# Eight lower halves of each weight formed on TensorE as a difference, and the second batch's variance on ScalarE

## The chip, the cores and the metric

One core of a Trainium2 chip runs the whole problem. The metric is the device time of one execution, in microseconds (us). Engines are named as the profile names them: PE (TensorE, with PEld for its weight loads), DVE (VectorE), ACT (ScalarE), POOL (GpSimd), SP (the queue that starts DMAs).

## The reference

Eight batches of landmark attention (8 heads, 576 tokens, 64 columns, 32 landmarks) are computed, their outputs laid side by side as x (576 x 512 per batch), and x goes through a Fourier mix and a two-layer perceptron:

```
mixed = real(fft(fft(x, axis=1), axis=2))
u  = x + mixed
un = (u - mean(u)) / sqrt(var(u) + 1e-6)          # per token
out = u + relu(un @ w_ch1) @ w_ch2                # 512 -> 2048 -> 512
```

## The kernel before, in words

Three Python generators write the program: `attention` (batch after batch), `weights` and `mlp`. A loop in `run` hands them control by a clock kept by cost estimates. PE executes in the order in which they write (L881); the order on DVE, ACT and POOL is made by the framework's scheduler. Each engine runs its list strictly in order, so an instruction that waits holds up all behind it.

**Weights.** w1 and w2 come as 64-bit floats and are cut into 16 pieces each, [128, 512]. For a piece, ACT makes the magnitude (`prepare`), DVE puts the number together in three instructions (L287 to L289), and ACT takes its maximum (`bound`). When a weight's 16 maxima are there, `scale` finds one power of two for it: a maximum on DVE, a transpose and a small product on PE, and five tiny DVE instructions that end in `wsc`. Then `halve` cuts each piece into an upper and a lower fp16 half (`split`, L209):

```
self.A.activation(hi, src, AF.Copy, scale=scale)                               # ACT
self.V.scalar_tensor_tensor(lo, src, scale, hi, ALU.mult, ALU.subtract)        # DVE
```

Piece f is kept as fp32 in slot f + 1 of `whole[w]`, and its two halves are written into slot f: the halves of piece f + 1 overwrite piece f, so ACT's hi of the next piece waits for DVE's lo of this one. w1 is halved while w2 is still being put together, one piece for one; w2 is halved after all that.

**Perceptron.** Tokens go in 18 chunks of 256. For a chunk, `mlp` runs eight steps over pairs of pieces of w1: 24 matmuls (three fp16 products of halves, 256 columns each) into a PSUM tile `h` of the pool `ps_h`, which has two banks (PSH = 2); ACT takes the relu's upper half out of it, DVE the lower (L852, L853). `second` then multiplies such a step's h with two pieces of w2: 12 matmuls of 512 columns into two accumulators `acc`. The first chunk needs a pair of w1 as soon as it is halved, and the second layer a pair of w2.

**Norm.** `norm` makes mean and variance of the u tiles: for batch 0 on ACT with sums that accumulate (`nm` is the negative mean), for all others on DVE with `bn_stats` and `bn_aggr`. Then come a power on POOL, un on DVE, its fp16 halves on ACT and POOL, and DMA transposes into unT.

Almost all instructions are recorded by one line (L121 for ACT, DVE and POOL, L197 for PE), so rows are told apart by tile names. `w<-w,wsc` is a half of a piece (hi on ACT, lo on DVE), `h<-h` and `mid<-h` empty a step of the perceptron, `w<-w,row`, `w<-big,row` and `row<-...` put pieces together.

Of the kernel before, what the change touches and what calls it, by code (L numbers as in the profile page):

```python
# [10 lines left out]
F32 = mybir.dt.float32  # L11
F16 = mybir.dt.float16
I32 = mybir.dt.int32
AF = mybir.ActivationFunctionType
ALU = mybir.AluOpType
AX = mybir.AxisListType

P = 128
H, S, D, LM, DM, DF = 8, 576, 64, 32, 512, 2048
NF = DF // P  # L20
# [105 lines left out]
class Kernel:  # L126
    def __init__(self, ctx, tc, NB, q, k, v, w1, w2, t1, t1t, t2, diag, mask, out):
        self.tc, self.nc, self.NB = tc, tc.nc, NB
        self.q, self.k, self.v, self.w1, self.w2, self.out = q, k, v, w1, w2, out
        nc = self.nc  # L130
# [10 lines left out]
        def const(src, shape, dtype, name):  # L141
            t = self.cp.tile(shape, dtype, name=name)
            nc.sync.dma_start(t, src)
            return t

        self.wraw, self.raw_there = [], []
        self.whole = [self.cp.tile([P, NF + 1, 512], F32, name=f"w{w}") for w in range(2)]
        self.mask = const(mask, [P, 6], F32, "mask")
# [7 lines left out]
        self.ones_bd = self.cp.tile([P, 4, 32], F32, name="ones_bd")  # L156
        nc.vector.tensor_copy(self.ones_bd, self.mask4.unsqueeze(2).broadcast_to([P, 4, 32]))
        self.mhalf = self.cp.tile([P, 2], F32, name="mhalf")
        nc.vector.memset(self.mhalf, -0.5)
# [73 lines left out]
    def weights(self):  # L233
        nc = self.nc
        V, A = self.V, self.A
        whole = self.whole
        slots = [[t[:, i] for i in range(NF + 1)] for t in whole]
        am = [self.cp.tile([P, NF], F32, name=f"wmax{w}") for w in range(2)]
        hl = [[t.bitcast(F16).rearrange("p (y m) -> p y m", y=2) for t in ss] for ss in slots]
        self.w1s = [t.rearrange("p y (c f) -> p y c f", c=KT) for t in hl[0]]  # L240
        self.w2s = hl[1]
        sc = self.cp.tile([P, 3], F32, name="wsc")
        pieces = [(w, f) for w in range(2) for f in range(NF)]
        mags = []
# [8 lines left out]
        def bound(i):  # L253

            w, f = pieces[i]
            A.activation(mags[i], slots[w][f + 1], AF.Abs, accum_out=am[w][:, f : f + 1])

        es = []

        def scale(w):  # L260
            a2 = self.small(1, "wm2")
            V.tensor_reduce(a2, am[w], AX.X, ALU.max)
            yield self.till(a2)
            e, r = yield from self.pow2(a2, 1, f"wp{w}")
            es.append(e)
            V.tensor_scalar(sc[:, w : w + 1], r[:, 0:1], (2.0**6, 2.0**14)[w], None, ALU.mult)

        def halve():
            w, f = pieces[sum(self.split_w)]
            self.split(hl[w][f][:, 0], hl[w][f][:, 1], slots[w][f + 1], sc[:, w : w + 1])  # L270
            self.split_w[w] = f + 1

        for i, (w, f) in enumerate(pieces):
# [11 lines left out]
            top, low = rv[:, :, 1], rv[:, :, 0]  # L285
            x, dst = mags[i].bitcast(I32), slots[w][f + 1]
            V.tensor_scalar(x, x, 3, None, ALU.logical_shift_left)  # L287
# [10 lines left out]
            if es:  # L298
                halve()
                yield max(0.0, max(self.V.free, self.G.free) - self.now - WT)  # L300
# [3 lines left out]
        self.inv2 = sc[:, 2:3]  # L304
        while sum(self.split_w) < 2 * NF:
            halve()
            yield max(0.0, max(self.V.free, self.A.free) - self.now - WT)
# [441 lines left out]
    def norm(self, b, uts):  # L749
        nc, V = self.nc, self.V  # L750
        n = len(uts)
        st, mv = self.sm.tile([P, 2, 6], F32, name="bn"), self.sm.tile([P, 2, 2], F32, name="mv")
        ve, r0, t, r1 = (self.small(2, x)[:, 0:n] for x in ("ve", "r0", "rt", "r1"))
        if b == 0:
            junk = self.row(512)
# [25 lines left out]
        for j, ut in enumerate(uts):  # L781
            i = self.ntile
# [10 lines left out]
            hl = self.row(1024, F16).rearrange("p (y d) -> p y d", y=2)  # L793
# [77 lines left out]
    def run(self):  # L871
# [3 lines left out]
        self.ulive, self.ufree, self.first_done, self.seconds, self.folded = 0, [], 0, 0, -1  # L875
        self.split_w, self.decoded = [0, 0], 0
        self.threads = []
# [83 lines left out]
```

## Time and profile before

| what | value |
|---|---|
| median of 3 runs | 1067.77 us (1065.95 to 1068.18) |
| the profiled execution, its time | 1067.68 us |
| its span, first to last instruction | 1065.9 us |
| PE busy | 981.1 us, 92% |
| DVE busy | 614.0 us, 58% |
| ACT busy | 351.7 us, 33% |
| mean granted PE clock | 0.96 |

Busy shares are means over stages that differ: PE is not full in the first 200 us and full from there on, while DVE is nearly full only in those first 200 us. The 1.8 us between time and span lie outside the instructions.

### The profile page before, as it was taken

What the parts mean: (1) busy time and instruction counts of PE and PEld (TensorE: products, weight loads), DVE (VectorE), ACT (ScalarE), POOL (GpSimd) and SP (SyncE); (2) the same over time, 40 slices, a digit from 0 to 9 for tenths busy, and PEclk for the clock granted to TensorE, in tenths of its full rate; (3) what the DMA queues carried; (4) which work ended last, traced back from release to release, by engine and by line L of the source; (5) the groups of instructions that cost most, each with busy time, mean ns of one, the idle gap of its engine ahead of it and who ended that gap; (6) DMA issues with size and microseconds to landing.
All of it is one profiled execution on the core that took longest, in us unless ns stands there. A gap on an engine that the chain in (4) does not pass through costs nothing.

```text
span 1065.9 us, 19548 instructions
## 1 busy us (share of the span) xinstructions
PE 981.1 (92%) x8008; PEld 681.0 (64%) x8008; DVE 614.0 (58%) x1655; ACT 351.7 (33%) x791; POOL 126.6 (12%) x137
## 2 busy tenths in 40 slices
PE   1553779999999999999999999999999999999998
PEld 0442645677776677766776777667766677766665
DVE  7889888768553476446746574567451654341111
ACT  4566755324221333124322332243312332111110
POOL 0101101021101030110302030104010030110000
PEclk8556989999999999999999999999999999999999
DMA  9824402221401022111502050114111010120000
GB/s 328 311 83 129 141 25 91 70 42 39 152 21 35 26 80 103 21 31 21 179 4 50 11 164 19 40 21 129 64 41 21 21 23 20 21 50 16 5 21 20
DMA packets 85994, 71.70 MB, mean 67 GB/s; under 512 B 56336, under 2 KB 74768, under 8 KB 85776
## 3 DMA queue, kind: packets, MB, share of 16 engines
q1 hardware_dynamic: 85904, 70.45, 22.1%
q8 instruction: 63, 1.03, 0.4%
q14 instruction: 27, 0.22, 0.1%
HBM read 48.02 MB, written 9.44 MB: 54 GB/s over the span
## 4 chain that ended last, share of the span: by engine, by line
PE 86%; DVE 8%; issue 2%; ACT 2%; DMA 1%; POOL 0%; SPq 0%; ACTq 0%; DVEq 0%
PE acc L197 34%; PE h L197 34%; PE at L197 16%; DVE w L121 2%; DVE row L121 2%; DVE mid L121 1%; PE at L202 1%; ACT row L121 1%; DVE lm L121 1%; DMA big<-q_dram 0%; ACT mid L121 0%; DVE asum L121 0%; DVE u L121 0%; DVE RE L121 0%; POOL row L121 0%
## 5 line engine op out<-in xcount | busy, mean ns | idle before, releaser
L197 PE MATMUL h<-unT,w 128*128 128x256 f16 x3456 | 413.5, 274 | 20.3 <-DMA unT<-row 11.5
L197 PEld LDWEIGHTS <-w 128*128 128x128 f16 x3456 | 336.2, 98 | 92.8 <-issue 19.5
L197 PE MATMUL acc<-w,h 128*128 128x512 f16 x1680 | 394.8, 379 | 0.0
L197 PEld LDWEIGHTS <-h 128*128 128x128 f16 x1680 | 161.9, 98 | 160.5 <-issue 3.4
L121 DVE SCALAR_TENSOR_TENSOR h<-h 128x512 f16<-128x512 f32 x140 | 96.5, 689 | 247.5 <-ACT h L121 247.0
L121 ACT ACTIVATE h<-h 128x512 f16<-128x512 f32 x140 | 83.4, 596 | 367.9 <-PE h L197 367.5
L121 POOL TENSOR_TENSOR r<-ve,mhalf 128x2 f32<-128x2 f32 (+1 forms) x20 | 13.7, 683 | 446.7 <-DVE ve L121 446.7
L121 POOL TENSOR_TENSOR row<-row 128x512 f16<-128x512 f32 (+1 forms) x44 | 47.3, 1089 | 44.0 <-ACT row L121 44.0
L197 PEld LDWEIGHTS <-mid 128*128 128x128 f16 x432 | 40.2, 103 | 17.7 <-issue 9.0
L197 PEld LDWEIGHTS <-big 128*128 128x128 f16 (+1 forms) x768 | 41.3, 106 | 13.6 <-issue 2.4
L121 POOL TENSOR_TENSOR mid<-mid,asum 128x512 f32<-128x512 f32 x14 | 15.1, 1080 | 272.2 <-issue 134.5
L121 DVE TENSOR_REDUCE lm<-big 128x32 f32<-128x576 f32 (+1 forms) x48 | 44.2, 945 | 3.3 <-DMA big<-k_dram 3.2
L121 DVE SCALAR_TENSOR_TENSOR row<-at,scw,row 128x262 f32<-128x262 f32 (+1 forms) x48 | 21.4, 486 | 41.4 <-ACT row L121 27.2
L121 ACT CAST row<-row 128x512 f16<-128x512 f32 (+1 forms) x44 | 23.2, 557 | 64.5 <-DVE row L121 63.9
L121 ACT ACTIVATE row<-w 128x512 f32<-128x512 f32 x54 | 33.8, 641 | 22.8 <-DVE w L121 12.4
L197 PE MATMUL at<-RE,E 128*128 128x96 f32 (+1 forms) x192 | 31.1, 288 | 9.0 <-DVE RE L121 9.0
L121 DVE SCALAR_TENSOR_TENSOR u<-at,scw,row 128x128 f32<-128x128 f32 (+3 forms) x120 | 38.9, 389 | 0.0
L121 POOL TENSOR_TENSOR mid<-mid 128x256 f32<-128x256 f32 (+1 forms) x32 | 31.5, 987 | 61.5 <-DVE mid L121 54.0
L197 PEld LDWEIGHTS at<-RE,E 128*128 128x128 f32 x192 | 28.6, 205 | 15.3 <-issue 6.2
L121 DVE TENSOR_TENSOR mid<-mid 128x256 f32<-128x256 f32 x48 | 34.5, 743 | 1.6 <-POOL mid L121 1.4
L197 PE MATMUL at<-mid,big 128*128 128x262 f16 (+1 forms) x288 | 34.3, 293 | 0.0
L121 DVE SCALAR_TENSOR_TENSOR u<-acc,wsc,u 128x512 f32<-128x512 f32 x36 | 26.7, 745 | 11.5 <-PE acc L197 11.3
(167 smaller groups left out, 955.6 us busy)
## 6 DMA issues: line engine op xcount, KB each, us to landing
w<-w_dram SPq DMA_DIRECT2D x22, 512.0 KB, 8.9
big<-v_dram SPq DMA_DIRECT2D x16, 640.0 KB, 9.2
big<-q_dram SPq DMA_DIRECT2D x16, 584.0 KB, 5.2
big<-k_dram SPq DMA_DIRECT2D x16, 576.0 KB, 4.2
out_dram<-u SPq DMA_DIRECT2D x36, 256.0 KB, 2.0
big<-w_dram SPq DMA_DIRECT2D x10, 512.0 KB, 8.2
unT<-row SPq DMA_TRANSPOSE x72, 2.4
t<-t_dram SPq DMA_DIRECT2D x1, 1048.0 KB, 9.2
```

The source lines that it names most:

```text
L121: return call(out, *args, **kw)
L197: self.nc.tensor.matmul(out, a, b, start=start, stop=stop, skip_group_check=True)
L202: self.nc.tensor.transpose(out, a, ident)
```

## The change

Pieces with an even number are halved as before. For an odd piece ACT makes hi, and PE forms the scaled difference in a tile of `ps_h`: the fp32 piece times the identity scaled by `wsc` (`scaled[w]`, tile `wid`), plus hi times minus the identity (`minus`, fp16). ACT copies that tile out as lo. For w1 the difference of an odd piece is written into the program one piece later (`left`), for w2 at once. w1's slots are one further apart (piece f in slot f + 2). Batch 1's mean and variance are made on ACT as those of batch 0.

```diff
@@ -144,7 +144,7 @@
             return t
 
         self.wraw, self.raw_there = [], []
-        self.whole = [self.cp.tile([P, NF + 1, 512], F32, name=f"w{w}") for w in range(2)]
+        self.whole = [self.cp.tile([P, NF + 2 - w, 512], F32, name=f"w{w}") for w in range(2)]
         self.mask = const(mask, [P, 6], F32, "mask")
         self.load(0)
         self.mask4, self.mask2 = self.mask[:, 0:4], self.mask[:, 4:6]
@@ -155,6 +155,8 @@
         nc.vector.memset(self.ones, 1.0)
         self.ones_bd = self.cp.tile([P, 4, 32], F32, name="ones_bd")
         nc.vector.tensor_copy(self.ones_bd, self.mask4.unsqueeze(2).broadcast_to([P, 4, 32]))
+        self.minus = self.cp.tile([P, P], F16, name="minus")
+        nc.vector.tensor_scalar(self.minus, self.ident, -1.0, None, ALU.mult)
         self.mhalf = self.cp.tile([P, 2], F32, name="mhalf")
         nc.vector.memset(self.mhalf, -0.5)
 
@@ -234,7 +236,7 @@
         nc = self.nc
         V, A = self.V, self.A
         whole = self.whole
-        slots = [[t[:, i] for i in range(NF + 1)] for t in whole]
+        slots = [[t[:, i] for i in range(NF + 2 - w)] for w, t in enumerate(whole)]
         am = [self.cp.tile([P, NF], F32, name=f"wmax{w}") for w in range(2)]
         hl = [[t.bitcast(F16).rearrange("p (y m) -> p y m", y=2) for t in ss] for ss in slots]
         self.w1s = [t.rearrange("p y (c f) -> p y c f", c=KT) for t in hl[0]]
...
-            A.activation(mags[i], slots[w][f + 1], AF.Abs, accum_out=am[w][:, f : f + 1])
+            A.activation(mags[i], slots[w][f + 2 - w], AF.Abs, accum_out=am[w][:, f : f + 1])
...
@@ -264,11 +266,33 @@
             e, r = yield from self.pow2(a2, 1, f"wp{w}")
             es.append(e)
             V.tensor_scalar(sc[:, w : w + 1], r[:, 0:1], (2.0**6, 2.0**14)[w], None, ALU.mult)
+            V.tensor_scalar(scaled[w], self.ident, sc[:, w : w + 1], None, ALU.mult)
+            self.begun[w] = 0
+
+        scaled = [self.cp.tile([P, P], F32, name=f"wid{w}") for w in range(2)]
+        left = []
 
         def halve():
-            w, f = pieces[sum(self.split_w)]
-            self.split(hl[w][f][:, 0], hl[w][f][:, 1], slots[w][f + 1], sc[:, w : w + 1])
-            self.split_w[w] = f + 1
+
+
+            w = 0 if self.begun[0] < NF else 1
+            f = self.begun[w]
+            hi, lo, src = hl[w][f][:, 0], hl[w][f][:, 1], slots[w][f + 2 - w]
+            if f % 2 == 0:
+                self.split(hi, lo, src, sc[:, w : w + 1])
+            else:
+                A.activation(hi, src, AF.Copy, scale=sc[:, w : w + 1])
+            self.begun[w] += 1
+            left.append((w, f, hi, lo, src))
+            while left and (left[0][1] % 2 == 0 or len(left) > 1 - left[0][0] or self.begun[0] == NF):
+                w, f, hi, lo, src = left.pop(0)
+                if f % 2:
+                    yield self.till(hi)
+                    ps = self.ps_h.tile([P, 512], F32, name="h")
+                    self.mm(ps, scaled[w], src, True, False)
+                    self.mm(ps, self.minus, hi, False, True)
+                    A.copy(lo, ps)
+                self.split_w[w] = f + 1
 
         for i, (w, f) in enumerate(pieces):
             while len(mags) < min(2 * NF, i + 1 + PREP):
...
-            x, dst = mags[i].bitcast(I32), slots[w][f + 1]
+            x, dst = mags[i].bitcast(I32), slots[w][f + 2 - w]
...
@@ -296,14 +320,14 @@
             if i == NF:
                 yield from scale(0)
             if es:
-                halve()
+                yield from halve()
                 yield max(0.0, max(self.V.free, self.G.free) - self.now - WT)
         bound(2 * NF - 1)
         yield from scale(1)
         V.tensor_scalar(sc[:, 2:3], es[0][:, 0:1], 2.0**-19, es[1][:, 0:1], ALU.mult, ALU.mult)
         self.inv2 = sc[:, 2:3]
-        while sum(self.split_w) < 2 * NF:
-            halve()
+        while sum(self.begun) < 2 * NF:
+            yield from halve()
             yield max(0.0, max(self.V.free, self.A.free) - self.now - WT)
 
     def arrival(self, mb):
@@ -751,7 +775,7 @@
         n = len(uts)
         st, mv = self.sm.tile([P, 2, 6], F32, name="bn"), self.sm.tile([P, 2, 2], F32, name="mv")
         ve, r0, t, r1 = (self.small(2, x)[:, 0:n] for x in ("ve", "r0", "rt", "r1"))
-        if b == 0:
+        if b < 2:
             junk = self.row(512)
             nm = self.small(2, "nm")[:, 0:n]
             for j, ut in enumerate(uts):
```

What follows are rows of the two programs' order. Numbers tell buffers apart; `w0_73` is the tile of w1's slots, `w1_74` that of w2's, `[waits ...]` names the engine (or DMA queue) whose signal an instruction waits for.

PE before, in the first chunk, from the end of one step of the first layer (`h_1079`) to the start of the next (`h_1116`):

```order
L197 LDWEIGHTS w0_73
L197 MATMUL h_1079<-unT_868,w0_73 128x256
L197 LDWEIGHTS w0_73 [waits Activation_49]
L197 MATMUL h_1116<-unT_868,w0_73 128x256 [waits DVE_49]
L197 LDWEIGHTS w0_73
L197 MATMUL h_1116<-unT_868,w0_73 128x256
```

PE of the changed kernel, at the same kind of place, from step `h_1200` to step `h_1243`:

```order
L199 LDWEIGHTS w0_73
L199 MATMUL h_1200<-unT_870,w0_73 128x256
L199 MATMUL h_1235<-w0_73,wid0_137 128x512 [waits DVE_49]
L199 LDWEIGHTS minus_108
L199 MATMUL h_1235<-w0_73,minus_108 128x512 [waits Activation_49]
L199 LDWEIGHTS w0_73
L199 MATMUL h_1243<-unT_870,w0_73 128x256 [waits DVE_49]
L199 LDWEIGHTS w0_73
L199 MATMUL h_1243<-unT_870,w0_73 128x256
```

A difference of 512 columns, in a tile of the same two-bank pool, now stands between any two steps of the first chunk.

ACT before, in the same stretch (`ACTIVATE w0<-w0,wsc` is a hi, `ACTIVATE row,wmax<-w1` a bound, `h<-h` a relu):

```order
L121 ACTIVATE row_1040,wmax1_133<-w1_74 128x512 [waits DVE_49]
L121 ACTIVATE h_1203<-h_1162 128x512 [waits PE_49]
L121 ACTIVATE w0_73<-w0_73,wsc_134 128x512 [waits DVE_49]
L121 ACTIVATE row_1087,wmax1_133<-w1_74 128x512 [waits DVE_49]
L121 ACTIVATE w0_73<-w0_73,wsc_134 128x512 [waits DVE_49]
L121 ACTIVATE h_1239<-h_1208 128x512 [waits PE_49]
```

ACT of the changed kernel there:

```order
L121 ACTIVATE mid_1183<-h_1151 128x512 [waits PE_49]
L121 ACTIVATE row_1094,wmax1_135<-w1_74 128x512 [waits DVE_49]
L121 CAST w0_73<-h_1188 128x512 [waits PE_49]
L121 ACTIVATE w0_73<-w0_73,wsc_136 128x512
L121 ACTIVATE w0_73<-w0_73,wsc_136 128x512 [waits DVE_49]
L121 ACTIVATE row_1141,wmax1_135<-w1_74 128x512 [waits DVE_49]
L121 ACTIVATE h_1230<-h_1200 128x512 [waits PE_49]
```

Between two relus ACT now also has a CAST that waits for a difference on PE.

PE of the changed kernel where w2 is halved and the second layer begins (`acc`), from the end of one pair to the start of the next:

```order
L199 MATMUL acc1_1426<-w1_74,mid_993 128x512
L199 MATMUL h_1501<-w1_74,wid1_138 128x512
L199 LDWEIGHTS minus_108
L199 MATMUL h_1501<-w1_74,minus_108 128x512
L199 LDWEIGHTS mid_1082
L199 MATMUL acc0_1425<-w1_74,mid_1082 128x512
```

Before, the 12 matmuls of one pair followed on those of the pair before; five of the eight differences of w2 now stand between such pairs, ahead of the products of the next batch's landmarks (`at<-big,qbd`), and three behind these, among the products of that batch's attention.

## Rows read from the trace of the kernel before

**Rows 1.** The page's part 2: tenths of busy time of PE and DVE, and of the granted PE clock, in 40 slices of the span (26.6 us each).

```profile
PE   1553779999999999999999999999999999999998
...
DVE  7889888768553476446746574567451654341111
...
PEclk8556989999999999999999999999999999999999
```

**Rows 2.** Busy time by stretch of the span: the stretch, its length, then busy us (and instructions) of PE, PEld, DVE, ACT and POOL, the granted PE clock, the DMA engines' share, GB/s.

```profile
110.00:125.00 15.00, 12.36 (x108) 10.42 (x109) 13.01 (x25) 11.82 (x23) 3.05 (x2) 1.00 0.63 174
125.00:140.00 15.00, 8.81 (x71) 6.34 (x72) 15.00 (x26) 11.46 (x24) 0.00 (x0) 1.00 0.32 109
140.00:147.00 7.00, 5.36 (x35) 3.85 (x32) 6.09 (x16) 0.88 (x3) 0.00 (x0) 0.75 0.00 0
147.00:167.00 20.00, 16.80 (x60) 6.62 (x62) 14.78 (x42) 11.12 (x18) 0.00 (x0) 0.75 0.10 30
167.00:190.00 23.00, 19.77 (x244) 13.14 (x242) 21.29 (x61) 12.80 (x32) 6.94 (x8) 1.00 0.25 79
190.00:215.00 25.00, 23.86 (x201) 16.82 (x201) 18.40 (x50) 9.95 (x26) 0.00 (x0) 1.00 0.23 74
215.00:1062.00 847.00, 845.43 (x6924) 588.39 (x6921) 432.37 (x1195) 229.33 (x512) 105.19 (x110) 1.00 0.17 47
```

**Rows 3.** DVE in order of time while w1 is halved: start, duration, instruction. A row's share of DVE is the distance to the next start.

```profile
122.05 0.68 DVE L121 SCALAR_TENSOR_TENSOR w<-big,row 128x512 int32<-128x512 int32 x1
122.67 0.75 DVE L121 SCALAR_TENSOR_TENSOR w<-w,wsc 128x512 f16<-128x512 f32 x1
123.34 0.76 DVE L121 TENSOR_SCALAR row<-row 128x512 int32<-128x512 int32 x2
124.01 0.69 DVE L121 SCALAR_TENSOR_TENSOR row<-big,row 128x512 int32<-128x512 int32 x1
124.61 0.69 DVE L121 SCALAR_TENSOR_TENSOR mid<-h,mid 128x512 f16<-128x512 f32 x1
```

**Rows 4.** PE in order of time, steps of the first chunk, with its idle time before a row and what ended it.

```profile
122.19 2.78 PE L197 MATMUL h<-unT,w 128*128 128x256 f16 x24 [0.69 <-DVE mid L121]
125.35 0.38 PE L197 MATMUL h<-unT,w 128*128 128x256 f16 x2 [0.38 <-DVE mid L121]
...
139.08 5.55 PE L197 MATMUL h<-unT,w 128*128 128x256 f16 x34 [2.52 <-DVE w L121]
```

**Rows 5.** Groups of instructions by their shapes over the whole span: count, busy us, mean ns of one, idle time before them.

```profile
L121 DVE SCALAR_TENSOR_TENSOR w<-w,wsc 128x512 f16<-128x512 f32 x32 | 24.8, 776 | 2.8 <-ACT w L121 2.8
L121 ACT ACTIVATE h<-h 128x512 f16<-128x512 f32 x140 | 83.4, 596 | 367.9 <-PE h L197 367.5
L121 DVE SCALAR_TENSOR_TENSOR h<-h 128x512 f16<-128x512 f32 x140 | 96.5, 689 | 247.5 <-ACT h L121 247.0
```

**Rows 6.** PE: sixteen fp32 passes of 288 columns (eight matmuls of two weight loads each, two at a time side by side on 64 weight columns), and, from the chain that ended last, 24 and 12 fp16 matmuls at full clock.

```profile
12.30 4.09 PE L197 MATMUL at<-big,qbd 128*64 128x288 f32 x16
...
166.81 2.16 PE L197 MATMUL at<-big,qbd 128*64 128x288 f32 x16
...
1046.45 2.62 PE h L197 x24
1049.07 2.59 PE acc L197 x12
```

**Rows 7.** ACT in order of time at the start of w2's halving.

```profile
147.56 0.72 ACT L121 ACTIVATE w<-w,wsc 128x512 f16<-128x512 f32 x1 [6.38 <-DVE wsc L121]
...
156.02 0.59 ACT L121 ACTIVATE klm<-lm,sc 128x64 f16<-128x64 f32 x2 [0.70 <-DVE sc L121]
156.52 1.44 ACT L121 ACTIVATE big<-big,sc 128x1024 f16<-128x1024 f32 x2
...
158.48 1.44 ACT L121 ACTIVATE big<-big,sc 128x1024 f16<-128x1024 f32 x2
```

**Rows 8.** The second layer's matmuls from 147 to 167 us: ns of the shortest, the median and the longest.

```profile
L197 PE MATMUL acc<-w,mid x48: 376/380/634, 148.3 to 165.9; 128*128 128x512 f16 x48
L197 PE MATMUL acc<-w,h x3: 379/379/379, 166.1 to 166.5; 128*128 128x512 f16 x3
```

**Rows 9.** The chain that ended last, from 167 to 188 us: the first and the last of the four lower halves in it.

```profile
168.50 0.67 DVE w L121
...
183.54 0.66 DVE w L121
```

**Rows 10.** The norm's instructions: on DVE (batches 1 to 7), and on ACT the sums of squares (batch 0); ns of the shortest, median and longest.

```profile
L121 DVE BATCH_NORM_STATS2 bn<-u x32: 673/685/695, 217.1 to 952.6; 128x6 f32<-128x512 f32 x32
L121 DVE BATCH_NORM_AGGREGATE mv<-bn x32: 163/182/183, 218.3 to 953.3; 128x2 f32<-128x6 f32 x32
...
L121 ACT ACTIVATE row<-u,nm x4: 706/707/723, 88.7 to 107.7; 128x512 f32<-128x512 f32 x4
L121 ACT ACTIVATION_READ_ACCUMULATOR row<-u,nm x4: 185/186/187, 89.3 to 108.3; 128x1 f32 x4
```

More of the change, by code (lines that the diff above doesn't have):

```diff
@@ L875, in run @@
         self.ulive, self.ufree, self.first_done, self.seconds, self.folded = 0, [], 0, 0, -1
-        self.split_w, self.decoded = [0, 0], 0
+        self.split_w, self.begun, self.decoded = [0, 0], [0, 0], 0
         self.threads = []
```

## The prediction

> **What bounds the kernel now.** I read the page's parts 1 and 2 first, then busy time by stretch, then single engines in order of time where no engine is full. The page shows two regimes [rows 1]: from the seventh slice on, at about 160 us, PE stands at 9 in all slices but the last, at full clock, while before that DVE stands at 7 to 9 and PE at 1 to 7. The table of stretches makes it sharp [rows 2]: from 215 to 1062 us PE is busy for 845.43 of 847 us. Whatever happens there to DVE or ACT gives at most the 1.6 us that are left; whatever is added there to PE comes out in full. So the end is the time at which PE becomes full, plus the PE work that is left then.
>
> Ahead of that lie two stages that the change touches. From about 90 to 147 us w2 is put together and w1 halved, and the first chunk's eight steps follow the halves. In its core DVE has no gap: 15.00 of 15 us from 125 to 140 [rows 2], and PE's waits there end on `w`, a half made by DVE [rows 4]. From 147 to 215 us w2 is halved, the second layer starts and the second batch's attention runs. There PE loses 3.20 us by idling from 147 to 167, 3.23 from 167 to 190 and 1.14 from 190 to 215, 7.6 in all [rows 2]; and its clock is at the lower of its two levels (1.2 instead of 2.4 GHz) for part of the time, 0.75 on the mean of the first 20 us. What that costs: 51 products of the second layer ran there [rows 8]; at full clock 12 take 2.59 us, 0.216 each [rows 6], so 51 take 11.0. With about 1.0 for the nine other instructions that makes 12.0, and PE was busy for 16.8 [rows 2]: 4.8 us. PE's loss from 147 to 215 is thus 12.4 us, the hole into which work of PE can fall for nothing.
>
> **The change, part by part.**
>
> *Sixteen subtractions leave DVE.* After a lower half's start at 122.67 the next instruction starts at 123.34 [rows 3], 0.67 us later. Eight of w1's are 5.4 us, eight of w2's as much.
>
> *Sixteen differences come to PE.* The trace has no fp32 matmul of 512 columns. The nearest is the row of 288 columns at full clock, 2.16 us for eight, two at a time, so four in a row [rows 6]. A 512-column fp16 product has 0.379 us from start to end [rows 8] and the next comes after 0.216, so some 0.16 of the 2.16 is the last one's way out; (2.16 - 0.16) / 4 = 0.50 us for 288 columns, 0.89 for 512. With the fp16 product of hi, 0.22, a difference is 1.11 us. The bounds are 1.18 (without taking off the way out) and, should it fall in an idle PE, 0; at the lower clock it is up to double, as the same eight take 4.09 us early on [rows 6].
>
> *Sixteen copies come to ACT.* A 128x512 read of PSUM to fp16 is the relu's 0.596 us [rows 5], 4.8 us for each weight. A hi stays what it is.
>
> *The first stage.* For w1 DVE gives up 5.4 us of its 28.0 from 110 to 140, and would have 22.6 left. But ACT has 23.3 there [rows 2], and 4.8 more make 28.1 of 30: now ACT is the fuller one, and alone allows 30 - 28.1 = 1.9 us. And each step's way is longer: a difference takes one of the two banks, so mostly the next step's 24 matmuls (2.62 us, [rows 6]) start only when the relu (0.60) and the subtraction (0.69, [rows 5]) have emptied the step before, 1.3 us in which PE has just the difference, 1.11, to do. 2.62 + 1.29 = 3.9 us is a step without any queueing, against some 4.4 of DVE work for a pair: two pieces at 0.34 + 0.60 + 0.60, one lower half of 0.67 and the subtraction of 0.60, all by distances of starts as in [rows 3]. Nothing is to spare there for an ACT that stands in a CAST, which waits for PE, with a relu behind it. Between a gain of 5.4 (all of DVE's) and a loss of as much as the relus are held up (0.6 us for each of seven handovers, 4.2), I take the halving of w2 to begin 0.4 us earlier than now, at 147.2 instead of 147.56 [rows 7]: most of the stage's gain is eaten.
>
> *The second stage.* Eight differences of w2 add 8 x 1.11 = 8.9 us to PE. How much falls into the hole of 12.4? A pair now goes: fp32 part 0.89; hi 0.72 [rows 7], which waits for it because it overwrites the piece that PE reads; the copy 0.60; then the eight products that need it, 8 x 0.216 = 1.73. That is 3.94 us, against 3.70 of pure PE work (2.59 + 1.11). Four pairs lose 1.0. Ahead of the first, PE waits for two hi and one lower half in a row, some 1.4 after its own fp32 part. ACT once has the second batch's landmarks and q to do in one go, 0.59 and twice 1.44 us [rows 7], with the copy of a pair behind them; of these 3.5 us about 1.2 reach PE. Makes 3.6 lost from 147 to 167, at full clock: PE is then at work some four fifths of the time in both stages, where it had 8.81 of 15 us ahead of the drop to 0.75 [rows 2]. From 167 to 215 PE lost 4.4; four lower halves, 2.7 us, stood in the chain there [rows 9], where the new order has two, and three differences fill gaps; I take 1.8. So 5.4 us of loss remain of 12.4, 7.0 us of the new work are free.
>
> *The second batch's variance.* Five tiles lose 0.685 + 0.182 on DVE, 4.3 us, and ACT gains two accumulating passes a tile, each near 0.71 + 0.19 [rows 10], 9 us. This is at 217 us and later, under PE's 845.43 of 847 us: nothing. Without that cover a norm of two tiles would come 1.9 us later (3.6 on ACT against 1.7 on DVE).
>
> *Small things.* The two scaled identities are one short DVE instruction each, minus identity one at the start under the loads; w1's slot that is further apart lets hi run ahead of the subtraction, which is in the first stage's figure.
>
> **Sum.** -0.4 + 8.9 - 7.0 = +1.5 us on the profiled execution's own 1067.68, that is 1069.2. The three runs' median is 1067.77, so nothing has to be shifted. 0.2%, 2.1 us, is about what a measurement of this kernel can tell from no change; the sum lies inside it.
>
> **The rivals.**
>
> *A: DVE's relief is handed on in full.* The trace speaks for it with the gapless DVE and with PE's waits on `w`; against it stands ACT's 28.1 of 30. Then w2's halving starts 5.4 us earlier: -5.4 + 8.9 - 7.0 = -3.5, 1064.2 us. Half of that gain would already bring -0.8.
>
> *B: the missing second bank.* In the first chunk a step waits for the emptying of the one before. If relu and subtraction each have to let one instruction of their queue finish first (0.6 us for a handover as the mean of both together), seven handovers cost 4.2 us instead of the gain of 0.4: +1.5 + 0.4 + 4.2 = +6.1, 1073.8 us. It decides from about 0.2 us a handover on. For it: DVE and ACT are both near full there. Against it: two of the steps start behind a difference's copy alone, and the order puts relus early. The Trainium skill, "Perfetto Trace Analysis", section on matmuls, asks for this case's opposite: independent groups should rotate through different PSUM banks so that one group's evacuation overlaps the next one's matmuls. The trace agrees as far as it shows the old order: with two banks PE idles for only 0.38 us between the steps at 122.19 and 125.35 [rows 4].
>
> *C: the clock stays low.* If w2's stage keeps its mean of 0.75, the 4.8 us are not given back: +6.3, 1074.0 us. For it: hi, lower half and copy still take turns with PE. Against it: PE is fuller ahead of this stage than it was. The Trainium skill, "Perfetto Trace Analysis", section on matmul optimizations, says that the engine scales its power with its utilization, so matmuls should run back to back; by that the fuller PE is the more likely one to keep its clock.
>
> **How the numbers follow.** The forecast has 0.38, A 0.30, B 0.18, C 0.14. A's whole range counts as faster; B and C as slower; of the forecast's own range, 1067 to 1071, the upper end is slower by a little: I give 0.36 to no change and 0.34 to slower. The time is the forecast's, 1069.2. The range runs from A's 1064.2, a little beyond for a cheaper difference, to B's and C's lower half, 1073.5; that leaves out about 2 in 10.
>
> **What will show it.** DVE's `w<-w,wsc` x16 instead of x32, and 16 casts on ACT of about 0.6 us. `h<-w,wid` near 0.9 us apart from its `minus`. In the first stage: ACT as full as DVE from 110 to 140, and PE waiting between steps for `h` or `mid` (the emptying) rather than for `w`; w2's first hi at 147 us. If that hi stands at 143 or earlier, A is right; at 150 or later, B. From 147 to 167: clock 1.00 and about 3.6 us idle; a clock of 0.75 again is C. From 215 us on nothing but a shift. What would make me wrong in kind is a PE that is not full after 215 us, because the order written by the cost estimates no longer fits.

## The result, and the profile after

The change made the kernel slower: 1075.12 us in the median (1074.64 to 1076.76, 4 runs) against 1066.86 (1065.36 to 1068.18, 4 runs) in the same comparison, a ratio of 1.0081 with an interval of 1.0061 to 1.0100. That is 8.3 us, where 1.5 had been forecast; 1075.1 lies above the forecast range's upper end of 1073.5. The profiled execution took 1074.75 us with a span of 1073.0, 7.1 us more than the span of before.

The page of after, its span and three rows of part 2 (as [rows 1]):

```profile
span 1073.0 us, 19679 instructions
...
PE   1555888899999999999999999999999999999998
...
DVE  7888957748553476526745575567551563441111
...
PEclk8668999999999999999999999999999999999999
```

DVE's row is lower from about 134 to 188 us, and PE's and the clock's are higher ahead of 160 us. But PE reaches its 9 only with the ninth slice, at about 215 us, where before it did with the seventh, at 160. So the page shows relief ahead of 160 us and a loss behind it. How large they are the stretches show (columns as in [rows 2]):

```profile
110.00:125.00 15.00, 11.25 (x67) 7.32 (x65) 13.05 (x26) 13.49 (x29) 2.27 (x2) 0.89 0.64 202
125.00:140.00 15.00, 13.12 (x96) 9.62 (x96) 13.23 (x27) 11.29 (x25) 0.00 (x0) 1.00 0.24 72
140.00:147.00 7.00, 5.92 (x50) 4.38 (x48) 3.65 (x17) 1.73 (x4) 0.00 (x0) 1.00 0.01 2
147.00:167.00 20.00, 18.02 (x79) 7.87 (x78) 10.49 (x29) 13.11 (x22) 0.00 (x0) 1.00 0.13 32
167.00:190.00 23.00, 19.19 (x239) 13.11 (x240) 18.27 (x59) 13.34 (x35) 6.92 (x8) 1.00 0.39 134
190.00:215.00 25.00, 21.70 (x161) 14.10 (x161) 18.60 (x52) 11.29 (x31) 0.00 (x0) 0.93 0.05 18
215.00:1069.00 854.00, 852.28 (x6966) 592.19 (x6963) 428.67 (x1183) 234.79 (x528) 104.92 (x110) 1.00 0.17 47
```

From 147 to 167 us PE now idles 1.98 us at a clock of 1.00, where before it idled 3.20 at 0.75 [rows 2]: the hole there was filled. From 167 to 215 it idles 3.81 and 3.30, 7.1 us, where before it was 3.23 and 1.14; and the clock is 0.93 in the last 25 us, which takes away about another 1.75 (0.07 of 25). Behind 215 us PE is full as before.

The new instructions have the forecast's price. The first row is the fp32 part, two records for each difference; the second is the copy on ACT (ns of the shortest, median and longest):

```profile
L199 PE MATMUL h<-w,wid x32: 592/592/697, 91.5 to 198.1; 128*128 128x512 f32 x32
L121 ACT CAST w<-h x16: 562/572/588, 94.0 to 199.0; 128x512 f16<-128x512 f32 x16
```

In order of time an fp32 part at 128.28 is followed by its fp16 product at 129.14, 0.86 us later (rows below); with 0.22 for that product a difference is 1.08 us of PE (forecast 1.11).

**How the runs below are read.** Three events cut each profile into parts: DVE writes w1's scale (`wsc<-wp_r`, first), then w2's scale (second), and PE starts the landmark product of the second batch, `at<-big,qbd` x16, with which the long chain of that batch's attention begins. The parts are called A (w1's scale to w2's), B (w2's scale to the product) and C (the product to the last instruction). In before the events stand at 90.86, 147.37 and 166.81 us, in the change at 89.02, 145.00 and 164.57. The first event moves between 88.8 and 91.2 us over the profiles of all kernels, also where the programs are the same up to there, and kernels of the same first stage have A's up to 1.3 apart: below that, one profile's A says nothing. The parts belong to one profiled execution, which need not be near its kernel's median: order_before's was the fastest of five (1071.47 us), change_bank's the slowest of six (1072.52). A ratio is the estimate from all runs of a comparison, against the kernel before in that comparison; it differs from the ratio of the two medians by up to 0.0013 (no_var).

| kernel | median, us | ratio and interval | A | B | C |
|---|---|---|---|---|---|
| before | 1066.86 | | 56.5 | 19.4 | 899.1 |
| the change | 1075.12 | 1.0081 (1.0061 to 1.0100) | 56.0 | 19.6 | 908.4 |
| var_only | 1065.93 | 0.9999 (0.9989 to 1.0008) | 55.5 | 19.2 | 899.1 |
| no_var | 1076.36 | 1.0085 (1.0071 to 1.0099) | 57.2 | 19.6 | 906.9 |
| w1_only | 1066.58 | 0.9997 (0.9987 to 1.0007) | 57.1 | 18.1 | 898.8 |
| w2_only | 1080.38 | 1.0127 (1.0112 to 1.0143) | 56.9 | 23.0 | 906.5 |
| slot_only | 1067.71 | 1.0014 (1.0005 to 1.0023) | 57.3 | 20.0 | 898.9 |
| w1_bank | 1058.46 | 0.9924 (0.9910 to 0.9938) | 50.5 | 18.5 | 898.9 |
| w1_wm | 1061.65 | 0.9950 (0.9938 to 0.9963) | 52.7 | 17.1 | 898.9 |
| w1_bank_wm | 1057.21 | 0.9923 (0.9908 to 0.9938) | 49.0 | 17.9 | 898.8 |
| before_wm | 1064.32 | 0.9989 (0.9979 to 0.9998) | 55.0 | 17.6 | 899.1 |
| order_before | 1073.37 | 1.0058 (1.0044 to 1.0072) | 58.2 | 22.0 | 900.1 |
| order_w2 | 1070.76 | 1.0039 (1.0024 to 1.0053) | 57.1 | 22.1 | 901.5 |
| w2_early | 1069.98 | 1.0037 (1.0025 to 1.0050) | 57.2 | 19.6 | 902.4 |
| w2_late | 1069.71 | 1.0033 (1.0021 to 1.0045) | 57.1 | 18.2 | 902.1 |
| early_order | 1070.59 | 1.0037 (1.0024 to 1.0050) | 58.8 | 20.7 | 898.8 |
| late_double | 1073.29 | 1.0061 (1.0047 to 1.0074) | 57.1 | 18.2 | 905.9 |
| change_bank | 1070.34 | 1.0044 (1.0027 to 1.0062) | 50.1 | 21.8 | 908.0 |
| change_bank_order | 1069.44 | 1.0033 (1.0021 to 1.0046) | 53.1 | 23.3 | 899.9 |

### The profile page after: what moved, and what is told of

Same layout as the page of the kernel before. It is cut to its first block, busy times and chain, and to the rows that moved or that the text cites. A ratio compares the mean times of both kernels' runs of the same rounds, so it can differ in the third digit from the quotient of the medians.

```text
span 1073.0 us, 19679 instructions
## 1 busy us (share of the span) xinstructions
PE 992.2 (92%) x8056; PEld 684.8 (64%) x8056; DVE 599.2 (56%) x1638; ACT 365.7 (34%) x827; POOL 126.5 (12%) x137
## 4 chain that ended last, share of the span: by engine, by line
PE 85%; issue 6%; DVE 5%; ACT 2%; DMA 1%; POOL 1%; SPq 0%; ACTq 0%; POOLq 0%
PE h L199 35%; PE acc L199 34%; PE at L199 15%; PE at L204 1%; DVE mid L121 1%; DVE row L121 1%; DVE w L121 1%; DMA big<-q_dram 1%; DVE lm L121 0%; POOL row L121 0%; ACT big L121 0%; ACT mid L121 0%; ACT w L121 0%; DVE u L121 0%; DVE h L121 0%
## 5 line engine op out<-in xcount | busy, mean ns | idle before, releaser
L121 ACT CAST row<-row 128x512 f16<-128x512 f32 (+1 forms) x44 | 23.3, 557 | 69.5 <-DVE row L121 68.2
```

What stands on the lines that cost most here:

```text
L121: return call(out, *args, **kw)
```

## The experiments

### The parts of the change alone

The variance on ACT for batch 1 alone, and the change without it:

```diff
-        if b == 0:
+        if b < 2:        # var_only: this line alone, in before; no_var: the change without it
```

> The kernel before with batch 1's variance on ScalarE and nothing else. The theory: no change, within 1 us of before. Rival: 2 to 4 us slower, from an unT that comes later or another written order.

> The change without the variance, which stays on DVE for batch 1. The theory: as the change, 1074.5 to 1076 us, since those passes run after 215 us under a PE that is full. Rival (the ten accumulating passes on ACT delay the second batch's unT or steer the order): 1070 to 1073.

var_only came out as the theory had it, 0.9999. no_var stands on the theory's side but 0.4 us above its range: 1.0085 without the variance against 1.0081 with it. The variance costs and gives nothing that these runs can tell.

Then the differences of one weight alone (`by_pe` decides for a piece, and the variance stays on DVE; w1's slots are those of the change in both; dots stand for lines that are not shown):

```diff
+        by_pe = lambda w, f: f % 2 and w == 0        # w1_only
+        by_pe = lambda w, f: f % 2 and w == 1        # w2_only
...
-            if f % 2 == 0:
+            if not by_pe(w, f):
                 self.split(hi, lo, src, sc[:, w : w + 1])
...
```

> Only w1's eight odd pieces are formed on PE; w2 is halved by DVE, the variance stays on DVE. The theory (the order): after's loss lies from 167 to 215 us, where w2's late differences hold back the second layer in the written order, so that the waits of the attention's chain find no filler; without them w2's halving starts some 2.4 us earlier (145.2 instead of 147.6) and that comes out whole or nearly: 1063.5 to 1065.5 us, 1.5 to 3.5 below before, and PE idles 4 to 5 us from 167 to 215 as in before. Rival (each difference costs PE its 1.1 us wherever it stands, since the order is fixed): eight of them give 1068 to 1071, slower by 1 to 4.

> Only w2's eight odd pieces are formed on PE; w1 with its slots as before halved by DVE (its slots one further apart, as in the change), variance on DVE. The theory: the loss of the whole change, and the first stage's gain of 2.4 missing: 1075 to 1078 us, 8 to 11 above before; h and acc steps missing ahead of 215 us, idle 6 to 8 us from 167 to 215. Rival (the variance or w1's part takes part in it): 1069 to 1072.

Neither expectation held. w1's differences alone changed nothing (0.9997). The expected gain of 2.4 us had been read from the change's own profile, where w2's first hi stands at 145.19; but no_var and w1_only, with the same program up to there, have A's of 57.2 and 57.1, so those 2.4 us were mostly an early start of that execution (w1's scale at 89.02 instead of 90.86). w2's differences alone cost 14.5 us, more than the whole change; B is longer there as well, 23.0 us, in which PE idles 4.0 at a mean clock of 0.88, where the change's B has 2.6 at 1.00. What causes this stays open. So the loss is w2's part, and it shows in C: every kernel in which w2 is halved as before has 898.8 to 899.1 there, the change has 908.4.

### Why w1's part gave nothing

```diff
-                    ps = self.ps_h.tile([P, 512], F32, name="h")
+                    ps = self.psum()                 # w1_bank: w1_only, tile from the attention's pool
```

> Only w1's differences, formed in a PSUM tile of the attention's pool, so that the steps keep their two banks. Theory (a step costs 4.28 us there: 2.62 + 1.07 + about 0.45 of waiting for the emptying of the step before and 0.14 of pipeline): the waits between steps go, the last step ends some 3 us earlier, but only the part behind the transpose of the maxima counts: 1063 to 1065.5. Rival (bank not the limit, a half's making is): same steps, 1066 to 1067.

w1_bank is w1_only with that one line, and PE's instructions stand in the same order in both. (The lists of ACT and DVE are made by the scheduler and differ from w1_only's in places, so what is measured is the line with all that follows from it.) It took 1058.46 us, a ratio of 0.9924 against w1_only's 0.9997: some 8 us, far beyond what was expected. By the parts of the two profiles it is 6.2 (A 6.7 less, B 0.4 more); 1.6 more are the earlier start of w1_bank's execution. In the change a step of the first chunk waits for the emptying of the one before (PE in order of time; the change as it was predicted):

```profile
125.67 2.78 PE L199 MATMUL h<-unT,w 128*128 128x256 f16 x24 [1.06 <-ACT w L121]
128.28 1.02 PE L199 MATMUL h<-w,wid 128*128 128x512 f32 x2
129.14 0.38 PE L199 MATMUL h<-w,minus 128*128 128x512 f16 x1
129.98 2.78 PE L199 MATMUL h<-unT,w 128*128 128x256 f16 x24 [0.46 <-DVE h L121]
...
134.26 2.78 PE L199 MATMUL h<-unT,w 128*128 128x256 f16 x24 [0.43 <-DVE h L121]
...
138.45 3.44 PE L199 MATMUL h<-unT,w 128*128 128x256 f16 x30 [0.33 <-DVE h L121]
141.72 0.27 PE L204 MATMUL at<-ident,wm 128*1 128x128 f32 x1
```

In w1_bank there is no wait on `h` or `mid` any more (PE in order of time):

```profile
116.24 2.92 PE L199 MATMUL h<-unT,w 128*128 128x256 f16 x24
119.00 1.02 PE L199 MATMUL at<-w,wid 128*128 128x512 f32 x2
119.86 0.38 PE L199 MATMUL at<-w,minus 128*128 128x512 f16 x1
120.08 3.07 PE L199 MATMUL h<-unT,w 128*128 128x256 f16 x24
...
132.72 3.44 PE L199 MATMUL h<-unT,w 128*128 128x256 f16 x30
136.00 0.27 PE L204 MATMUL at<-ident,wm 128*1 128x128 f32 x1
```

Where two steps follow one another without a wait they are 3.84 us apart (116.24 to 120.08), where the bank is missing 4.3 (129.98 to 134.26). The groups of PE from 108 to 136 us say what went: idle time ahead of the steps, first in w1_only, then in w1_bank.

```profile
L199 PE MATMUL h<-unT,w 128*128 128x256 f16 x121 | 15.9, 291 | 4.7 <-ACT w L121 4.0 <-DVE h L121 0.4 <-DVE mid L121 0.2
```

```profile
L199 PE MATMUL h<-unT,w 128*128 128x256 f16 x174 | 21.0, 273 | 1.6 <-ACT w L121 1.5
```

The larger part is put down to ACT's copies (4.0 us), in two waits. But at both, the subtraction that empties the step before ended at almost the same time as the copy (PE, DVE and ACT of w1_only):

```profile
113.42 1.02 PE L199 MATMUL h<-w,wid 128*128 128x512 f32 x2
117.58 4.36 PE L199 MATMUL h<-unT,w 128*128 128x256 f16 x24 [2.92 <-ACT w L121]
...
128.33 2.78 PE L199 MATMUL h<-unT,w 128*128 128x256 f16 x24 [1.13 <-ACT w L121]
```

```profile
116.77 0.67 DVE L121 SCALAR_TENSOR_TENSOR mid<-h,mid 128x512 f16<-128x512 f32 x1
...
127.55 0.68 DVE L121 SCALAR_TENSOR_TENSOR mid<-h,mid 128x512 f16<-128x512 f32 x1
```

```profile
116.95 0.58 ACT L121 CAST w<-h 128x512 f16<-128x512 f32 x1
...
127.71 0.57 ACT L121 CAST w<-h 128x512 f16<-128x512 f32 x1
```

The subtractions end at 117.44 and 128.23, the copies at 117.53 and 128.28, the steps start at 117.58 and 128.33. By the subtraction alone they could have begun at most 0.14 us earlier: these are waits for the emptying as well. The first of them shows how long an emptying can take when relu and subtraction stand behind other work in their lists: the difference behind the step starts at 113.42, so the step itself is done soon after, and its bank is free 4 us later. With the bank given back, the waits for copies shrink to 1.5. A falls from 57.1 to 50.5, and w2's scale stands at 139.31 us:

```profile
139.31 0.15 DVE L121 TENSOR_SCALAR wsc<-wp_r 128x1 f32<-128x1 f32 x1
```

Of the 9.2 us between the spans of before and w1_bank, A gives 6.0 and B 0.9; 2.0 are an early start of this execution. So both rivals A and B of the prediction were true at once: DVE's relief is worth some 6 us, and the missing second bank ate it. The Trainium skill, "Perfetto Trace Analysis", section on matmuls, asks that independent groups rotate through different PSUM banks; the runs agree, with 6 to 8 us for that one line.

A second thing held up w2's scale. With DVE relieved, w2's maxima (`wm`) are ready well before PE takes their transpose, which stands behind most of the last step in PE's order: in the change DVE has them at 134.3 us, and the transpose starts at 141.72 (the last row of the change's PE above).

```profile
134.28 0.17 DVE L121 TENSOR_REDUCE wm<-wmax 128x1 f32<-128x16 f32 x1
```

In w1_wm the last step is written behind it:

```diff
             for i in range(NF // 2):
+                while ch == 0 and i == NF // 2 - 1 and self.topped == 0:   # set by scale(1)
+                    yield 0.3
```

> Only w1's differences, and the first chunk's last step is written behind the transpose of w2's maxima (it stood ahead of it). Theory (w1's relief of DVE is real, the maxima are there at 136.9 us, but their transpose waits in PE's order for the last step until 144.4): w2's halving starts 3 to 5 us earlier after its w1 scale than in the kernel with w1's differences alone, and 2 to 4 us of it reach the end: 1062.5 to 1064.5. Rival (what comes behind is bound by something else, the attention's chain or DVE): no change, 1065.5 to 1067.

> The kernel before, with nothing but the last step of the first chunk written behind the transpose of w2's maxima. Theory (in before DVE has the maxima only at 141.5 us, 2.4 us after PE began the last step, so there is little to take): within 1.5 us of before. Rival (the 4 us of the same edit with w1's differences came from the order alone): 1062 to 1064.

> Only w1's differences, in the attention's banks, and the last step of the first chunk written behind the transpose of w2's maxima. Theory (both gains are cuts of the same way from w1's last half to w2's scale; in the kernel with the bank alone the transpose stood at 136.0 with DVE's maxima a little earlier): 1056 to 1058.5 us. Rival (PE's order has the maxima late no more, so nothing is left of it, and the last step comes later): 1058 to 1060.

(`topped` is 0 at the start and 1 when the program has come to w2's maxima.) w1_wm gave 0.9950, a little more than expected, and A fell to 52.7. In before the same edit gave 0.9989, 1.45 us by the medians and so just inside the theory's 1.5: there DVE is late itself. The two edits together are no sum, though the time lies in the range that the theory gave: 0.9923 against 0.9924 for the bank alone, since with the bank the last step and with it the transpose come early anyway.

The slots of w1, which moved apart with its differences, have no part in it: slot_only is before with the slots of after.

> The kernel before with w1's slots one further apart, and no difference on PE, variance on DVE. Theory (ACT's hi ran ahead of DVE nowhere on the path): within 1 us of before. Rival (part of what w1's differences bring in the attention's banks is the slot's): 2 us or more faster.

It was 1.8 us slower (1.0014), a little outside the bound, but nothing of the 2 us or more that the rival had.

### Why w2's part costs so much

Two things could be behind C's 9.3 us: the differences' own work, or the order in which the program is written. The clock of cost estimates charges each difference for its matmuls and a wait for hi (`till`), so the weights' generator falls behind in it: w2's last piece is halved at 176.1 us of that clock in the change and at 148.7 in before, as the expectation of order_w2 has it (the clock of estimates is in no trace). The second layer's products, and the second chunk's steps behind them, then stand later in PE's order relative to the attention's chain. order_before leaves the differences out of the clock's account, order_w2 only the wait for a hi of w2:

```diff
-                    yield self.till(hi)
+                    now = self.now                    # order_before
                     self.mm(ps, scaled[w], src, True, False)
                     self.mm(ps, self.minus, hi, False, True)
-                    A.copy(lo, ps)
+                    self.now = now
+                    nc.scalar.copy(lo, ps)
+                    V.free = max(V.free, now) + 0.07 + 1.04e-3 * 512
...
```

> The change whole (sixteen differences and the variance), but the clock of cost estimates is kept as if DVE still formed every lower half: the differences take none of its time, so first steps, second-layer products and the attention's chain are written in the order of before, with the differences between them. Theory (the written order loses the fillers): the products and steps done by 215 us come back to within a third of before, PE idles 4 to 5 us from 167 to 215, and the time falls to 1067 to 1070.5 us. Rival (the differences' own 8.9 us on PE and their waits for hi are the loss, whatever the order): 1073.5 us or more.

> The change whole, but in the clock of cost estimates a difference of w2 does not wait for its hi (on the chip it does). In that clock w2's last half then stands at 162.0 instead of 176.1 (before: 148.7). Theory (order): about half of the way back, 1070 to 1073 us. Rival (differences' own cost): 1074 or more, since PE now also waits in place for each hi.

C went back to 900.1 and 901.5, as the order's theory has it. The time did not follow as far: 1.0058 and 1.0039, so 2 to 4.5 of 8.3 us came back; order_w2 lies in its range, order_before missed it from above and ended at the rival's edge. A part of what was taken from C came back in B, 22 us instead of 19.6: in these orders a sixth difference (1.08) and three products of the second layer (0.65) stand ahead of the landmark product, 1.7 of the 2.4 us. Order_before has about 1 us more in A besides. Of the two differences that are left behind the product there, with 2.2 us of work, C shows only 1.0: in the order of before, about half of it does fall into gaps.

How C looks from inside is seen in the first 48 us behind the product (columns as in [rows 2]), in before, the change and w2_early:

```profile
166.81:214.81 48.00, 43.63 (x443) 29.99 (x443) 39.50 (x110) 22.94 (x58) 6.94 (x8) 1.00 0.24 77
```

```profile
164.57:212.57 48.00, 40.62 (x393) 26.21 (x393) 37.21 (x110) 24.55 (x61) 6.92 (x8) 0.96 0.21 71
```

```profile
165.73:213.73 48.00, 41.58 (x429) 28.70 (x429) 39.86 (x109) 23.28 (x59) 7.34 (x8) 1.00 0.23 77
```

The change has 7.38 us of idle PE there against 4.37, 3.0 more; a clock below 1.00, the 1.75 us from above; three differences, 3.2; and three products of the second layer that before had done ahead of the landmark product, 0.65. That is 8.6 of the 9.3. In no_var the clock stayed at 1.00, and C was 1.5 us shorter: the low clock is not in every execution of this order. w2_early, without a difference there, has 6.42 us idle, 2.0 more than before, and the three products. Where the idle time stands is seen in order of time. Before, in two places of the chain:

```profile
187.76 0.69 PE L197 MATMUL at<-RE,E 128*128 128x96 f32 x4 [1.03 <-DVE RE L121]
188.28 1.47 PE L197 MATMUL h<-unT,w 128*128 128x256 f16 x12
189.59 0.62 PE L197 MATMUL at<-RE,E 128*128 128x96 f32 x4
190.05 0.82 PE L197 MATMUL h<-unT,w 128*128 128x256 f16 x6
...
205.06 2.78 PE L197 MATMUL h<-unT,w 128*128 128x256 f16 x24
207.77 1.20 PE L197 MATMUL at<-t,Wt 128*64 128x262 f16 x18
```

And the change, in the same chain:

```profile
178.70 1.02 PE L199 MATMUL h<-w,wid 128*128 128x512 f32 x2
179.56 0.38 PE L199 MATMUL h<-w,minus 128*128 128x512 f16 x1
180.97 0.66 PE L199 MATMUL at<-RE,E 128*128 128x96 f32 x4 [1.03 <-DVE RE L121]
181.46 2.75 PE L199 MATMUL acc<-w,h 128*128 128x512 f16 x12
184.05 0.58 PE L199 MATMUL at<-RE,E 128*128 128x96 f32 x4
185.72 0.69 PE L199 MATMUL at<-RE,E 128*128 128x96 f32 x4 [1.08 <-DVE RE L121]
...
195.24 0.27 PE L204 MATMUL at<-ident,wm 128*1 128x128 f32 x1 [1.16 <-DVE big L121]
...
197.04 0.83 PE L199 MATMUL h<-unT,w 128*128 128x256 f16 x6
...
201.81 1.48 PE L199 MATMUL at<-t,Wt 128*64 128x262 f16 x18 [1.55 <-ACT Wt L121]
```

Before puts steps of the second chunk between products of the chain, so PE works while DVE makes the next `RE` and ACT the next `Wt`. In the change the first matmuls of such a step stand at 197.04, because by the code `mlp` first writes the products of the pairs at hand, and waits for w2's halves to exist in the clock of estimates. The waits of the chain ahead of it (1.08 and 1.16) and behind it (1.55) stay open.

The next runs split the eight by their place: only pieces 1 to 9, ahead of the product, or only 11, 13 and 15, behind it.

```diff
+        by_pe = lambda w, f: f % 2 and (w == 0 or f < 10)    # w2_early
+        by_pe = lambda w, f: f % 2 and (w == 0 or f > 10)    # w2_late
```

> The change whole, except that w2's pieces 11, 13 and 15 are halved by ACT and DVE as before: only w2's first five differences are left. From the second batch's landmark product (at<-big,qbd) to the end the trace of before takes 899.1 us, of the change 908.4. Theory (the late three, by their place and by what they hold back in the order, are the loss; the first five fall into idle time and a low clock): that stretch falls to 900 to 903, and the time to 1067.5 to 1070. Rival (the order is displaced by all eight, since each delays the weights in the clock of cost estimates): 905 or more, and 1072 to 1075.

> The change whole, except that of w2 only pieces 11, 13 and 15 are formed on PE; 1 to 9 are halved by ACT and DVE. Theory (the late three are the loss): from the landmark product to the end 905 to 908 us, time 1071 to 1075. Rival (all eight displace the order): 901 to 904, 1068 to 1071.

By its numbers w2_early went with the theory and w2_late with the rival, so neither has it whole: each half costs C about 3 us, 902.4 and 902.1, and together they cost 9.3 (7.8 in no_var); what makes up the rest stays open, but for the lower clock. The first five do it with no difference behind the product, so it can't be their own work there. Ahead of the product they are cheap. The kernel to compare with is w1_only, which has the same first stage and none of them:

```profile
147.59:165.70 18.11, 14.19 (x55) 5.48 (x54) 13.51 (x39) 10.43 (x17) 0.00 (x0) 0.91 0.10 33
```

```profile
145.00:164.57 19.57, 16.95 (x65) 7.20 (x65) 10.70 (x34) 12.37 (x22) 0.00 (x0) 1.00 0.10 30
```

This is B in w1_only, then in the change. With 5.4 us of differences it is 1.5 longer, and 0.65 of products have gone to C: the five cost some 2 us, because they take the place of idle time (3.9 us there, 2.6 in the change) and the clock is higher. Two more runs tell what the 3 us in C are:

> The change with only w2's first five differences (pieces 11, 13 and 15 on ACT and DVE), and the clock of cost estimates kept as if DVE formed every lower half, so that the order is that of before. With the change's own order this kernel took 902.4 us from the landmark product to the end. Theory (its 3.3 us there are displacement of the order alone, no difference stands there): 899 to 900 us. Rival (late copies or hi on ACT, or a changed state of the queues, cost them): 902 or more. Ahead of the product, from w2's scale, 19 to 22 us; in all 1066.5 to 1070.

> The change with only w2's last three differences on PE, each of them computed twice into the same tile (two more matmuls of each kind; the second pass overwrites the first), in an unchanged order. With single ones this stretch took 902.1 us, 3.0 more than in before. Theory (a difference in the attention's stretch costs its whole 1.08 us of PE, since the idle gaps there stand elsewhere, ahead of what waits for the chain): 3.2 more, 905.3 us, and 1072 to 1073.5 in all. Rival (they stand in gaps and only the order costs): 902 to 903, and 1069.5 to 1070.5.

Both theories held for C. With the order of before the first five leave C at 898.8: their 3.3 us there were displacement alone. Doubled late differences cost 3.8 more (905.9), slightly over their price of 3 x 1.08: in the change's order a difference behind the product costs its whole PE time.

But early_order was no faster than w2_early in all, 1.0037 both and 0.6 us above its range: A and B are longer, 58.8 and 20.7. One plain reading of the total is thus not excluded. Against w1_only the span of the change is 8.5 us longer (1073.0 to 1064.5), and eight differences are 8 x 1.08 = 8.6 us of PE work: in sum w2's differences cost their own time, and what the first five gain ahead of the product is lost behind it. That the order decides where the loss stands is shown; that another order would save it is shown only as far as order_w2's 4.4 us and order_before's 1.8.

### Bank and order mended together

> The change whole, only the differences' PSUM tile comes from the attention's pool instead of the steps' pool. Theory (two separate things: w1's part is worth 8 us once the steps keep both banks; w2's part costs 8 to 9.5 us wherever w2's halving begins): the sum, 1066 to 1069 us, as before or up to 0.2% slower. Rival (the bank was w2's trouble too, since chunk 1's steps share it): 1060 to 1064.

> The change whole, with the differences' tile from the attention's pool and the clock of cost estimates kept as if DVE formed every lower half. Theory (bank 8 us, order 2 to 5 us, independent): 1062 to 1065 us, faster than before, but slower than w1's part alone with its bank (1058.5), since w2's differences still cost 3 to 5. Rival (with bank and order mended the differences of w2 are free): 1058 to 1060.

Both are misses, slower than expected. With the bank, A falls by 6 us as in w1_bank, but B is 21.8: PE idles even less there than in the change (1.84 us against 2.62), but its clock is 0.84 instead of 1.00, which over 21.8 us is 3.5. The five differences are no longer cheap. With the order of before C is mended (899.9), but A gives back 3 us and B has 23.3. The differences of w2 thus still cost some 11 us against w1_bank. The six runs of change_bank lie in two groups, 1068.1 to 1069.0 and 1071.7 to 1072.5, the profile in the upper; what parts them stays open. So does which wait lengthens A in the orders of before (58.2 and 58.8 against 57.1, and with the bank 53.1 against 50.1).

The versions that beat both kernels by more than 0.2% have only w1's differences. The simplest of the fastest is w1_bank: w1's eight differences on PE in a bank of the attention's pool, w2 halved as before, 1058.46 us; w1_bank_wm (1057.21) is no different by its ratio.

## Why the prediction was wrong, step by step

- **The price of a difference** (1.11) was right, 1.08; so was the copy's (0.60, measured 0.57). PE is full behind 215 us, as said, and the variance is free under it.
- **The first stage** (-0.4) came out near enough in sum: w1's part alone changed nothing, and A is 57.1 where before has 56.5. The forecast's reason was right too, that a step now waits for the emptying of the one before. What it didn't see is how large the two sides were: a gain of some 6 us and a loss as large. Rival B gave the loss 4.2 us and 0.18 of the chance, as an alternative to A, where both were at work. The rows of before already spoke for it: the prediction has PE's waits end on `w`, but two of the three in [rows 4] end on `mid`, the emptying. Its loads missed as well: from 110 to 140 us DVE has 26.3 us, where 22.6 were forecast, and ACT 24.8, where 28.1 were.
- **147 to 167 us** (3.6 of loss left at full clock) was right in kind and even better: 1.98 us idle, clock 1.00. Rival C, the clock that stays low, fell here; w1_only, with a clock of 0.91 in B and none of w2's differences, shows that a part of the rise comes with w1's.
- **167 to 215 us** is the step that failed: "three differences fill gaps; I take 1.8". Measured are 7.1 us of idle time and 1.75 of lower clock. The difference to 1.8, 7.0 us, less the 1.6 won ahead of it, is the miss (5.4 of the 5.6 between +1.5 and the spans' +7.1): of the new work not 7.0 us were free but 1.6. The step read the gaps of before as room and took PE's order around them as given. But that order comes from the clock of cost estimates, and the change moves the weights' generator in it by 27 us. The gaps were not filled; the work that had filled their neighbours was moved away from them (the 3.3 us of w2_early's C, which are gone in early_order), and the late differences cost their whole time (late_double). The lower clock of 190 to 215 us, which the forecast didn't have, stood in one execution and not in no_var's; its cause stays open.
- The prediction had named it as what would make it wrong in kind, a PE that no longer fits the written order, but placed that behind 215 us, where nothing happened.

## What to carry to other kernels

Idle time on an engine is only room for new work if the new work stands there in the engine's order, and if it doesn't push away what already fills the neighbouring gaps; where a cost model writes the order, ask first what the change does to the model's clock. Before a result is drawn into a pool that others rotate through, count who still has a second bank: here one line was worth 6 to 8 us. And a change of two parts should be timed in parts: one half of this one is worth some 8 us against before once it has its bank, the other costs as much or more.

## What the runs showed of the hardware that was not expected

Five fp32 differences, 5.4 us of PE work, cost only some 2 us ahead of the landmark product: PE's granted clock was higher together with them, 1.00 in the change's B against 0.91 in w1_only's, and they filled idle time. In change_bank, where A is 5.9 us shorter than in the change, the clock in B was 0.84 with the same differences, and B was 2.2 us longer. What decides between the two levels there no run shows.
